# Picking the first expert's rows with matrix products instead of a gather, and loading the sink values without their zeros

## The chip, the cores and the metric

The kernel runs on one core of one Trainium2 chip. The metric is the device time of one execution in microseconds, from the first to the last instruction of the program with what the device adds around them. Each engine works through its own list of instructions in order: TensorE (PE), VectorE (DVE), ScalarE (ACT), GpSimd (POOL), and SyncE (SP), which only issues transfers.

## The reference

Three stages follow each other, and each one's output is the next one's input.

```python
# attention: B=2, H=8, S=768, D=64; 4 sink positions, window 128
scores = scale * np.matmul(q, k.transpose(0, 1, 3, 2))
keep = is_sink | in_window
scores = np.where(keep, scores, -1000000000.0)
a = softmax(scores);  attn_out = np.matmul(a, v)          # -> x, 1536 tokens x 512
# mixture of experts with a capacity: E=8, cap = 1536 // 8 = 192
logits = x @ w_gate
order = np.argsort(-logits.flatten())
for idx in order:
    tok, e = (int(idx) // E, int(idx) % E)
    if assigned[tok] >= 0 or counts[e] >= cap:
        continue
    assigned[tok] = e
    counts[e] += 1
for e in range(E):
    mask = assigned == e
    out[mask] = np.maximum(x[mask] @ w1[e], 0.0) @ w2[e]  # 512 -> 1024 -> 512
# dense layer over all tokens: 512 -> 2048 -> 512, w_in and w_out given in float64
h = x @ w_in
g = np.maximum(h, 0.0) + alpha * np.minimum(h, 0.0)
return (g @ w_out).astype(np.float32)
```

## The kernel before

**Who sets the order.** Every piece of work is a `task` of a planner (`Plan`) with a cost for each engine that may do it, what it reads and writes, and extra urgency (`urge`, `boost`). The planner simulates the engines, starts the most pressing ready task, and so writes out each engine's fixed order before the kernel is built. `lag` and `tail` are delays it assumes. Buffers come from rings (`Ring`); a task that wants a buffer waits until the last user of one is done.

**Attention.** 1536 tokens are 12 blocks of 128 (6 per batch element). The values lie in `vraw` (12 blocks of 128x512 float32, from `v` in four loads). Before a batch element's values can be used, the largest absolute value of its six blocks is taken, one block at a time (`vmax`): by ACT at L407 for the blocks in `BY_ACT`, else by DVE at L409. From it comes a power-of-two scale `svf` (and its inverse `isv`), and the values are split into a float16 high part and a float16 rest. The values of the four sinks arrive as `vsr`, laid out with one 65-wide column group per head on a block diagonal that is mostly zeros, and are split at L454 (ACT) and L458 (DVE). Each finished block of attention output `x` goes to DRAM (`xd`) and, scaled and split into `x16` (float16 high and rest, a ring of two buffers), to a transposed copy for the gate; the last two blocks (`TURNED`) are turned by TensorE instead, and split at L619 (ACT) and L621 (DVE).

**Routing.** It goes one expert after the other, `s` = 0 to 7. A phase (`closing`, then `phase`) finds each token's best expert left (row maximum `m`, L1067; one-hot `oh`, L1071), spreads the row maxima over all partitions (12 TensorE transposes of a broadcast column, L1096, copied by ACT at L1100), compares all tokens with all (`cm`, L1116 to L1131, in phase 1 for three blocks in a lent buffer that the trace calls `gt`; some of the comparisons start on ACT or POOL at L1121 and are finished by DVE at L1127 and L1131), and counts with TensorE (L1163, 144 products of 8 columns for 12 blocks). The threshold follows (`both`, `red`, transposes `total` at L1182), then the ranks `rk` and the tokens that are gone. Phase 0 runs inside attention, in two groups of blocks. The phases are chained: each takes the tokens that the one before left.

**Fetching an expert's rows** (`hot`, `gather`). DVE writes a one-hot table `ohs` of the expert's 192 places over the 12 blocks of tokens (L1266, 12 instructions of 128x192, float16). For experts 0 and 1, TensorE multiplies it with the token numbers (`tok`, one column each, L1425), DVE turns the sums into integers `sidx` (L1439, L1440), and POOL issues two indirect transfers that fetch the 192 rows from `xd` into `xg` (L1446). TensorE turns them (8 transposes, L1459) and ACT copies them to `xT` (L1463). `busy` (L1356) and `keep_busy` put products of 512 columns without use into the time in which TensorE waits for expert 0's rows: three of them and six.

**The rest.** An expert's first layer is 8 products of 4 matmuls (L1574, float32, which the trace lists as two rows each; `raw` are its weights), its second layer eight more of the same form; experts 4 to 7 use float16 parts (L1581). After every second expert comes a share of the dense layer (`chunk`, L1708 and L1751). Its weights w_in and w_out arrive as float64 bits in a ring of three (`r`), and are turned into float32 `w` in 34 buffers by ACT, DVE and POOL, a conveyor that runs from the routing on.

## Time and profile before

| | |
|---|---|
| runs | 609.23, 609.66, 613.13 us; median 609.66 us |
| profiled execution | 608.75 us; its span 607.0 us |
| mean granted clock of TensorE | 0.955 of full speed |
| PE busy | 559.9 us (92%), 4532 matmuls; weight loads beside them 410.0 us (68%) |
| DVE busy | 461.2 us (76%), 1299 instructions |
| ACT busy | 357.7 us (59%), 742 instructions |
| POOL busy | 161.0 us (27%), 247 instructions |

The shares are means over stages that differ: attention until about 97 us, the routing of the first two experts with the first expert's products until about 176 us, and from then on experts and dense layer. So the tables by stage and the chains of waits say more than the shares.

### The profile page before, as it was taken

The page shows a single profiled execution, that of the slowest core. Times are in us where ns is not written, and L with a number is a line of the kernel's source. Part 1 is how long each engine was busy: PE and PEld are TensorE (multiplying, and loading weights), DVE is VectorE, ACT ScalarE, POOL GpSimd, SP SyncE. Part 2 cuts the span into 40 slices and gives each one's busy share as a digit, 9 for nine tenths or more (in the row PEclk, how much of TensorE's full clock was granted, in tenths as well). Part 3 has the DMA queues.
Part 4 walks back from the last instruction along what each step waited for, and adds up shares of the span by engine and source line. Part 5 has one row for each costly group of instructions (what it writes and reads, how often), then busy time and mean ns, then how long its engine had stood idle before and what let it go on. Part 6 is the DMA issues. An engine that isn't in the chain of part 4 may idle for free.

```text
span 607.0 us, 12432 instructions
## 1 busy us (share of the span) xinstructions
PE 559.9 (92%) x4532; PEld 410.0 (68%) x4532; DVE 461.2 (76%) x1299; ACT 357.7 (59%) x742; POOL 161.0 (27%) x247
## 2 busy tenths in 40 slices
PE   5899997659789999999899999999999999899995
PEld 3567675449688668888898555598755559855552
DVE  6989987858647898998699998989987657743231
ACT  6778888357457967866665553566344446542222
POOL 4867835230643321436301201000220000020002
PEclk9789998569889999999999999999999999999998
DMA  8845354264868536343554448464697155210001
GB/s 282 295 104 134 100 87 140 50 219 116 305 183 280 205 105 209 97 138 107 153 164 157 131 144 309 164 195 153 196 321 256 39 169 166 80 43 10 1 0 53
DMA packets 40555, 91.99 MB, mean 152 GB/s; under 512 B 16703, under 2 KB 17230, under 8 KB 40398
## 3 DMA queue, kind: packets, MB, share of 16 engines
q1 hardware_dynamic: 37710, 84.27, 44.3%
q0 software_dynamic: 2784, 6.93, 3.3%
q8 instruction: 36, 0.59, 0.4%
q14 instruction: 25, 0.20, 0.1%
HBM read 82.15 MB, written 6.41 MB: 146 GB/s over the span
## 4 chain that ended last, share of the span: by engine, by line
PE 47%; issue 12%; DVE 11%; ACT 8%; DMA 4%; POOL 1%; another core or an unknown queue 0%; POOLq 0%; SPq 0%; ACTq 0%
PE o L1751 14%; PE h L1708 13%; PE h L1574 8%; PE h L1581 8%; DMA xg<-xd,sidx 3%; DVE spl L1559 1%; DVE cm L1116 1%; PE r L1163 1%; DVE cm L1131 1%; ACT w L860 1%; PE r L1459 1%; ACT spl L1557 1%; ACT cm L1121 1%; DVE w L900 1%; DMA L<-cd 1%
## 5 line engine op out<-in xcount | busy, mean ns | idle before, releaser
L1751 PE MATMUL o<-w,gt 128*128 128x512 f16 x432 | 101.9, 379 | 0.0
L1708 PE MATMUL h<-x,w 128*128 128x384 f16 x576 | 100.7, 326 | 0.0
L1708 PEld LDWEIGHTS <-w 128*128 128x128 f16 x576 | 55.8, 98 | 40.6 <-issue 0.5
L1721 ACT ACTIVATE t<-h,slope 128x384 f32<-128x384 f32 x64 | 37.0, 578 | 72.3 <-PE h L1708 72.2
L1751 PEld LDWEIGHTS <-gt 128*128 128x128 f16 x432 | 41.3, 98 | 43.3 <-issue 0.5
L1581 PEld LDWEIGHTS <-spl 128*128 128x128 f16 x768 | 63.4, 98 | 3.2 <-issue 2.6
L1724 DVE SCALAR_TENSOR_TENSOR v<-h,way,t 128x384 f32<-128x384 f32 x61 | 37.3, 612 | 35.3 <-ACT t L1721 35.3
L907 POOL TENSOR_TENSOR w<-w,sg 128x512 f32<-128x512 f32 x22 | 28.8, 1310 | 88.8 <-DVE w L900 29.0
L1574 PE MATMUL h<-xT,raw 128*128 128x192 f32 x256 | 48.1, 338 | 2.3 <-DVE x L1625 1.8
L1446 POOL DMA_INDIRECT xg<-xd,sidx x16 | 20.6, 1286 | 100.5 <-DVE sidx L1440 62.4
L1574 PE MATMUL h<-h,raw 128*128 128x192 f32 x256 | 46.4, 339 | 0.4 <-DVE x L1625 0.4
L506 ACT ACTIVATE P<-sm,mn 128x260 f32<-128x260 f32 (+1 forms) x96 | 42.7, 491 | 4.7 <-DVE mn L495 4.6
L1797 POOL DMA_INDIRECT out<-ot,sidx x9 | 8.9, 990 | 136.2 <-ACT ot L1788 97.4
L1574 PEld LDWEIGHTS h<-xT,raw 128*128 128x128 f32 x256 | 42.5, 194 | 3.4 <-DVE x L1625 2.1
L1574 PEld LDWEIGHTS h<-h,raw 128*128 128x128 f32 x256 | 43.5, 198 | 1.1 <-DVE x L1625 0.6
L1559 DVE SCALAR_TENSOR_TENSOR spl<-raw,es,spl 128x1024 f16<-128x1024 f32 x32 | 40.7, 1280 | 4.5 <-ACT spl L1557 4.4
L1728 ACT CAST gt<-v 128x384 f16<-128x384 f32 x48 | 24.5, 510 | 28.9 <-DVE v L1724 27.5
L485 PE MATMUL s<-k,q 64*128 64x260 f32 (+1 forms) x192 | 36.8, 457 | 4.4 <-DMA q<-qT 4.1
L495 DVE CUSTOM_DVE_ANT_0 sm<-s,mask 128x260 f32<-128x260 f32 (+1 forms) x96 | 35.7, 397 | 4.1 <-PE s L485 3.8
L1729 DVE TENSOR_TENSOR gt<-v,gt 128x384 f16<-128x384 f32 x48 | 26.5, 553 | 13.7 <-ACT gt L1728 13.6
L1557 ACT ACTIVATE spl<-raw,es 128x1024 f16<-128x1024 f32 x32 | 36.4, 1143 | 0.0
L1581 PE MATMUL h<-xT,spl 128*128 128x192 f16 x384 | 33.5, 246 | 1.5 <-DVE h L1604 1.2
(291 smaller groups left out, 1241.5 us busy)
## 6 DMA issues: line engine op xcount, KB each, us to landing
raw<-w SPq DMA_DIRECT2D x96, 512.0 KB, 4.6
r<-w_in SPq DMA_DIRECT2D x16, 512.0 KB, 8.1
r<-w_out SPq DMA_DIRECT2D x16, 512.0 KB, 4.4
vraw<-v SPq DMA_DIRECT2D x4, 768.0 KB, 8.5
xd<-x SPq DMA_DIRECT2D x12, 256.0 KB
k<-kT SPq DMA_DIRECT2D x11, 260.0 KB
q<-qT SPq DMA_DIRECT2D x11, 256.0 KB, 2.8
vsr<-vs SPq DMA_DIRECT2D x1, 780.0 KB
```

What stands on the lines that cost most here:

```text
L485: nc.tensor.matmul(s.tile[:, :n].rearrange("p (j k) -> p j k", k=KW), lhsT=qs[t].tile[half, p], rhs=kk, start=True, stop=True)
L495: task({"DVE": dve(n)}, lambda: nc.vector.tensor_tensor_reduce(out=sm.tile[:, :n], in0=s.tile[:, :n], in1=mask[:, :n], scale=-0.125, scala ...
L506: task({"ACT": act(n) + 0.137}, lambda h=h, sm=sm, mn=mn: nc.scalar.activation(P[t].tile[:, h, :n], sm.tile[:, :n], AF.Exp, bias=mn.tile, ...
L907: (nc.gpsimd if e == "POOL" else nc.vector).tensor_tensor(x.tile, x.tile, sg.tile, OP.mult)
L1557: task({"ACT": act_sb(1024) + 0.09}, lambda: nc.scalar.activation(v(0), src(), AF.Copy, scale=scale()), r=[raw, ws], w=[b.part(0)], lag=se ...
L1559: task({"DVE": dve(1024) + 0.2}, lambda: nc.vector.scalar_tensor_tensor(v(1), src(), scale(), v(0), OP.mult, OP.subtract), r=[raw, ws, b.p ...
L1574: nc.tensor.matmul(ps.tile[:, 0:CAP], lhsT=w[:, k], rhs=x, start=first and k == 0, stop=last and k == 3, skip_group_check=True)
L1581: nc.tensor.matmul(ps.tile[:, 0:CAP], lhsT=w[:, i, k], rhs=xs()[k][:, j], start=first and n == 0, stop=last and n == len(ways) - 1, skip_g ...
L1708: nc.tensor.matmul(ps.tile[:, 0:CH], lhsT=w[:, i, k], rhs=y[j][:, k], start=(n == 0), stop=(n == len(ways) - 1))
L1721: task({"ACT": act(CH)}, lambda: nc.scalar.activation(t.tile, ps.tile[:, 0:CH], AF.Copy, scale=slope), r=[ps, wres], w=[t])
L1724: task({"DVE": dve(CH) + 0.065}, lambda: nc.vector.scalar_tensor_tensor(to(), ps.tile[:, 0:CH], way, t.tile, OP.mult, OP.max), r=[ps, t, w ...
L1751: nc.tensor.matmul(ops[t].tile, lhsT=gv[:, i, sl], rhs=wv[:, j], start=(f == n == 0), stop=(f == FB - 1 and n == 2))
```

## The change

1. The value tile `vraw` outlives attention. Once a block's values are used up, its slot takes the float16 parts of that block's attention output, in place of the ring `x16`. The last two blocks, whose split went to the transposed copy alone, are split into their slots too (`lower`: L669 on ACT, L672 on DVE; the latter not before the comparisons of phase 0 are done).
2. Expert 0's rows are not gathered (`BY_PE`). 96 matmuls (L1444: weights 128x128 from `vraw`, the one-hot table of 192 columns as the moving side; 12 blocks x 2 parts x 4 column groups) add up in four banks of PSUM, two for each batch element, and L1454 (ACT, times `isv[0]`, then DVE, times `isv[1]` and added) writes `xT`. The index products of expert 0 stay, for the later scatter, with a delay of 20 us in the plan. The products without use go.
3. The sink values come without the zeros (`vs` 1/8 of the size) after the gate weights in SP's order (`ORDER`: k, q, two loads of values, w, s), and are spread on the chip with a mask `own` (a tensor product on DVE or POOL) after the split.
4. All twelve maxima of the values prefer ACT (`BY_ACT`).
5. Phase 1's row maxima and their broadcast get the urgency that phase 0's had (`soon`), expert 1's gather is planned with 4.0 us instead of 2.2 (`tail`).
6. The `w` ring takes 22 buffers of its own and the 12 slots of `vraw` once they are free (`lend`).

```diff
+class Kept(Buf):
...
+        self.tile = tile
...
+    def lend(self, kept):
+        self.pools += [k.tile for k in kept]
+        self.past += kept
...
-ORDER = "k q a b s w"
+ORDER = "k q a b w s"
...
-BY_ACT = (0, 1, 3)
+BY_ACT = tuple(range(12))
...
+def halves(tile):
+
+    return tile.bitcast(F16).rearrange("p (a d) -> p a d", a=2)
...
-    vraw = cst.tile([128, NBLK, DM], F32, name="vraw")
...
-    vsr = cst.tile([96, B, 2, H, D + 1], F32, name="vsr")
+    vsr = cst.tile([96, B, 2, D + 1], F32, name="vsr")
+    vsd = cst.tile([96, B, 2, D + 1], F16, name="vsd")
+    own = cst.tile([96, H], F16, name="own")
...
-    k_res, v_res = [Res() for _ in range(NBLK)], [Res() for _ in range(NBLK)]
+    k_res, v_res = [Res() for _ in range(NBLK)], [Kept(vraw[:, t]) for t in range(NBLK)]
...
-        load(lambda: nc.sync.dma_start(out=vsr, in_=vs), [vs_res], 1 << 19)
+        load(lambda: nc.sync.dma_start(out=vsr, in_=vs), [vs_res], 1 << 17)
...
+    own_res = Res()
+    task({"DVE": 0.2}, lambda: nc.vector.tensor_reduce(
+        own, ident[0:96, 0:96].rearrange("p (r h x) -> p h r x", r=3, h=H), AX.XY, OP.max), w=[own_res])
...
-            nc.scalar.activation(vsh[:, b, :, :, 0:D], vsr[:, b, :, :, 0:D], AF.Copy, scale=svf[b][0:96])
-            nc.scalar.copy(vsh[:, b, :, :, D:D + 1], vsr[:, b, :, :, D:D + 1])
-
-        task({"ACT": 1.1}, first, r=[vs_res, sv_res[b]], w=[vsh_res[b]])
-        task({"DVE": 1.15}, lambda: nc.vector.scalar_tensor_tensor(
-            vsh[64:96, b, :, :, 0:D], vsr[64:96, b, :, :, 0:D], svf[b][64:96], vsh[64:96, b, :, :, 0:D],
-            OP.mult, OP.subtract), r=[vs_res, sv_res[b]], w=[vsh_res[b]])
+            nc.scalar.activation(vsd[:, b, :, 0:D], vsr[:, b, :, 0:D], AF.Copy, scale=svf[b][0:96])
+            nc.scalar.copy(vsd[:, b, :, D:D + 1], vsr[:, b, :, D:D + 1])
+
+        def rest():
+            nc.vector.scalar_tensor_tensor(vsd[64:96, b, :, 0:D], vsr[64:96, b, :, 0:D], svf[b][64:96], vsd[64:96, b, :, 0:D],
+                                           OP.mult, OP.subtract)
+
+        def spread(e):
+            (nc.vector if e == "DVE" else nc.gpsimd).tensor_tensor(
+                vsh[:, b], vsd[:, b].unsqueeze(2).to_broadcast([96, 2, H, D + 1]),
+                own.unsqueeze(1).unsqueeze(3).to_broadcast([96, 2, H, D + 1]), OP.mult)
+
+        dense = Res()
+        task({"ACT": 0.4}, first, r=[vs_res, sv_res[b]], w=[dense])
+        task({"DVE": 0.25}, rest, r=[vs_res, sv_res[b]], w=[dense])
+        task({"POOL": 2.3, "DVE": 1.2}, spread, r=[dense, own_res], w=[vsh_res[b]])
...
-        task({"SP": 0.06}, lambda: nc.sync.dma_start(out=xd[block(t) * 128:(block(t) + 1) * 128, :], in_=x.tile), r=parts,
+        task({"SP": 0.06}, lambda: nc.sync.dma_start(out=xd[n * 128:(n + 1) * 128, :], in_=x.tile), r=parts,
...
+            late.append(lambda after: lower(t, after))
             return
-        x16, xs, xT = r_x16.new(), r_xs.new(), r_xT.new()
-        task({"ACT": 0.613}, lambda: nc.scalar.activation(x16.tile[:, 0], x.tile, AF.Copy, scale=svf[b]),
-             r=[*parts, sv_res[b]], w=[x16.part(0)])
+        x16 = lower(t)
+        task({"SP": 0.06}, lambda: nc.sync.dma_start_transpose(
+            out=xT.tile.rearrange("p a c k -> p (a c) k"), in_=x16.rearrange("p a d -> p (a d)")),
+            r=[v_res[n]], w=[xT.part(0), xT.part(1)], tail=2.8)
+
...
+        task({"ACT": 0.613}, lambda: nc.scalar.activation(x16[:, 0], x.tile, AF.Copy, scale=svf[b]),
+             r=[*parts, sv_res[b]], w=[own])
+        if t >= NBLK - TURNED:
+            task({"DVE": 0.67}, lambda: nc.vector.scalar_tensor_tensor(x16[:, 1], x.tile, svf[b], x16[:, 0], OP.mult, OP.subtract),
+                 r=parts, w=[own], after=after)
+            return
...
+        task({"POOL": 1.12}, lambda: nc.gpsimd.tensor_tensor(x16[:, 1], xs.tile, x16[:, 0], OP.subtract),
+             r=[xs], w=[own])
+        return x16
...
-                        vs[r, h, g, s, :, par, h, :D] = v[:, h, n, :]
+                        vs[r, h, g, s, :, par, :D] = v[:, h, n, :]
...
-        self.ring = Ring(ctx.enter_context(self.tc.tile_pool(name="w_cst", bufs=1)), "w", [128, DM], F32, 2 * FB + self.MORE)
+    def room(self, ctx, kept):
+        self.ring = Ring(ctx.enter_context(self.tc.tile_pool(name="w_cst", bufs=1)), "w", [128, DM], F32, 2 * FB + self.MORE - C)
+        self.ring.lend(kept)
...
-    FILL = 6
...
+    BY_PE = (0,)
+    PICK, SET = 300.0, 2000.0
...
-            soon = 2000.0 if s == 0 else 0.0
+            soon = 2000.0 if s == 0 else 2000.0 if s == 1 else 0.0
...
+        self.compared = task({"DVE": 0.35 * nb / C + 0.25}, thresholds, r=[*counted, far, *mm], w=[both, red])
+        seq.append(self.compared)
...
-        def keep_busy(after):
-
-            ps, last = r_h.new(), None
-            for _ in range(self.FILL):
-                last = task({"PE": 0.35}, lambda: nc.tensor.matmul(
-                    ps.tile, lhsT=self.ones, rhs=self.ones[:, 0:1].to_broadcast([128, 512]), start=True, stop=True,
-                    skip_group_check=True), w=[ps] if last is None else (), after=[last] if last else [after], boost=-1000.0)
...
+        def chosen(s, o, parts):
+            a = s % 2
+            xT = xTs[s] = r_xT.new()
+            banks = [[r.new() for h in range(2)] for r in (r_h, r_o)]
+            got = {(b, h): [] for b in range(2) for h in range(2)}
+            begun = set()
...
+                            b, rows = c // NB, halves(x16[c].tile)
+                            for k in range(2):
+                                for i in range(2):
+                                    at = (2 * h + k) * 128
+                                    nc.tensor.matmul(banks[b][h].tile[:, k * CAP:(k + 1) * CAP], lhsT=rows[:, i, at:at + 128],
+                                                     rhs=o.tile[:, c, a], start=(b, h) not in begun,
+                                                     stop=(c % NB == NB - 1 and k == i == 1), skip_group_check=True)
+                                    begun.add((b, h))
+
+                    task({"PE": 0.083 * 4 * len(cs)}, pick, r=[ro, *[x16[c] for c in cs]], w=[got[b, h][-1] for b in to], urge=self.PICK)
+            for h in range(2):
+                view = lambda b, h=h: banks[b][h].tile[:, 0:CH].rearrange("p (k t) -> p k t", k=2)
+                task({"ACT": act(CH)}, lambda h=h, v=view: nc.scalar.activation(
+                    xT.tile[:, 2 * h:2 * h + 2], v(0), AF.Copy, scale=isv[0]), r=[*got[0, h], sv_res[0]], w=[xT.part(h)], urge=self.SET)
+                task({"DVE": dve(CH) + 0.065}, lambda h=h, v=view: nc.vector.scalar_tensor_tensor(
+                    xT.tile[:, 2 * h:2 * h + 2], v(1), isv[1], xT.tile[:, 2 * h:2 * h + 2], OP.mult, OP.add),
...
-                             w=got[-1:], pre=busy(ips) if x == 0 else None)
-            if s == 0:
-                keep_busy(named)
...
+            if s in self.BY_PE:
+                chosen(s, o, parts)
...
+                    w=[to], tail=4.0 if s < 2 else 6.0)
             xT = xTs[s] = r_xT.new()
             src, pss = [], []
...
         L = logits[:, :, 0:E]
+        vraw = g.tile([128, C, DM], F32, name="vraw")
...
-            r_s, last = attention(tc, nc, plan, part, a["qT"], a["kT"], a["v"], a["vs"], a["wg"], xd, x_blocks, L, l_blocks,
-                                  n_sink, window, ident, identh)
-            routed.begin(part, r_s, GROUPS, [last])
+            r_s, last, late, x16, *back = attention(tc, nc, plan, part, a["qT"], a["kT"], a["v"], a["vs"], a["wg"], xd, x_blocks, L,
+                                              l_blocks, n_sink, window, ident, identh, g, vraw)
...
         weights.ways()
-        routed.build(ctx, a["w1"], a["w2"], weights, out)
```

On DVE, between the threshold of phase 0 and the one-hot table of expert 0, there stood before (`tot`, `mx`, `sm`, `ei`: the expert's total and name; `rf`, `rk`: ranks):

```order
L1203 TENSOR_TENSOR rf_2662<-qm_2648,sm_2654 128x96
L1204 TENSOR_REDUCE rk_2663<-rf_2662 128x12
L1210 SCALAR_TENSOR_TENSOR L<-sm_2654,L 128x12x8
L1208 SCALAR_TENSOR_TENSOR dead<-rk_2663,dead 128x12
L1266 TENSOR_SCALAR ohs_2726<-slots,rk_2663 128x192 x12
L1067 TENSOR_REDUCE m_2761<-L 128x12
L784 TENSOR_SCALAR way<-al 128x16
L785 TENSOR_SCALAR way<-way 128x16
L786 TENSOR_TENSOR slope<-way,al 128x16
L1070 SCALAR_TENSOR_TENSOR m_2776<-dead,m_2761 128x12
L1071 TENSOR_TENSOR oh_2777<-L,m_2776 128x96
```

and now, first where the threshold is formed, then at the table:

```order
L1239 SCALAR_TENSOR_TENSOR qm_2645<-oh_2257,s_2404 128x96
L672 SCALAR_TENSOR_TENSOR vraw<-x_2233,scv_167,vraw 128x512
L1231 TENSOR_REDUCE tot_2649<-s_2404 8x1
L672 SCALAR_TENSOR_TENSOR vraw<-x_2347,scv_167,vraw 128x512
L1083 TENSOR_REDUCE mx_2654<-s_2404 128x1
```

```order
L1258 SCALAR_TENSOR_TENSOR L<-sm_2653,L 128x12x8
L1256 SCALAR_TENSOR_TENSOR dead<-rk_2662,dead 128x12
L1114 TENSOR_REDUCE m_2725<-L 128x12
L1314 TENSOR_SCALAR ohs_2729<-slots,rk_2662 128x192 x4
L1117 SCALAR_TENSOR_TENSOR m_2739<-dead,m_2725 128x12
L1118 TENSOR_TENSOR oh_2740<-L,m_2739 128x96
L1314 TENSOR_SCALAR ohs_2729<-slots,rk_2662 128x192 x8
```

Two 128x512 operations have come in between the steps of the threshold, and phase 1's `m` and `oh` have moved ahead of the table's last eight blocks.

On PE, at the start of expert 0's rows, there stood the last index products, phase 1's broadcasts, six products without use (the last of the three before the index products stand further up), and then the turning of the gathered rows:

```order
L1425 MATMUL r_2737<-tok,ohs_2726 64x1
L1096 MATMUL r_2782<-ident,m_2761 128x128 x4
L1096 MATMUL r_2796<-ident,m_2761 128x128 x4
L1096 MATMUL r_2804<-ident,m_2761 128x128 x4
L1356 LDWEIGHTS ones
L1356 MATMUL h_2815<-ones 128x512
```

and now the broadcasts come right behind the threshold's last transpose, and the picks behind them:

```order
L1229 MATMUL s_2404<-ident,red_2641 8x128
L1233 MATMUL s_2404<-ident,tot_2649 128x8
L1143 MATMUL r_2734<-ident,m_2725 128x128 x4
L1143 MATMUL r_2743<-ident,m_2725 128x128 x4
L1143 MATMUL r_2757<-ident,m_2725 128x128 x4
L1444 LDWEIGHTS vraw
L1444 MATMUL h_2766<-ohs_2729,vraw 128x192
```

The 96 picks follow each other without anything between them, then 72 counts of phase 1 (L1210) ahead of expert 0's first product, where 36 stood before; L1454's two operations on DVE stand behind some twenty comparisons of phase 1 and conversions of `w`. The gathered rows of expert 1 are turned behind the first five products of expert 0's second layer, as before.

On ACT, early in attention, there stood before (`P`: the exponentials, `pth`: a copy of their transposes):

```order
L506 ACTIVATE P_340<-sm_325,mn_326 128x260
L407 ACTIVATE junk,mx<-vraw 128x512 x2
L506 ACTIVATE P_340<-sm_334,mn_335 128x260
L506 ACTIVATE P_340<-sm_342,mn_343 128x260
L506 ACTIVATE P_340<-sm_352,mn_353 128x260
L407 ACTIVATE junk,mx<-vraw 128x512
```

and now:

```order
L537 ACTIVATE P_343<-sm_328,mn_329 128x260
L429 ACTIVATE junk,mx<-vraw 128x512 x3
L537 ACTIVATE P_343<-sm_337,mn_338 128x260
L429 ACTIVATE junk,mx<-vraw 128x512 x3
L537 ACTIVATE P_343<-sm_345,mn_346 128x260
```

The eight maxima that DVE did have come to stand on ACT between the exponentials.

## Rows read from the trace of the kernel before

**Rows 1.** Table by stretch; columns: stretch, length, PE, PEld, DVE, ACT, POOL, PEclk, DMA, GB/s

```profile
10.00:30.00 20.00, 15.80 (x116) 10.07 (x114) 19.55 (x73) 15.93 (x37) 11.99 (x14) 0.84 0.90 302
119.00:137.00 18.00, 11.33 (x89) 8.92 (x89) 11.44 (x41) 8.69 (x15) 6.01 (x3) 0.59 0.58 197
161.00:176.00 15.00, 10.36 (x48) 9.97 (x47) 2.87 (x6) 4.32 (x11) 11.23 (x21) 0.77 0.57 190
205.00:290.00 85.00, 83.20 (x566) 68.14 (x565) 77.42 (x186) 60.64 (x128) 31.54 (x31) 1.00 0.41 128
```

**Rows 2.** The chain that ended last, 119 to 176 us; start, length, what

```profile
119.18 2.24 DVE ohs L1266 x12
...
123.19 10.41 DMA xg<-xd,sidx
133.64 2.09 PE h L1459 x8
...
136.68 2.77 PE h L1574 x8
...
146.54 1.41 PE h L1574 x8
...
156.75 7.78 DMA xg<-xd,sidx
164.57 1.76 PE r L1459 x7
166.32 9.34 PE h L1574 x40
```

**Rows 3.** Waits of PE, 100 to 200 us, and of DVE, from 119 us: us, times, longest

```profile
PE h L1459 <- DMA xg<-xd,sidx: 6.5, 1, 6.5
PE r L1459 <- DMA xg<-xd,sidx: 3.5, 1, 3.5
...
DVE gt L1127 <- ACT gt L1121: 5.3, 1, 5.3
```

**Rows 4.** Timeline of PE: start, length, instruction

```profile
122.62 2.96 PE L1096 MATMUL r<-ident,m 128*128 128x128 f32 x12
145.50 1.04 PE L1163 MATMUL r<-oh,cm 128*128 128x8 bf16 x36
153.44 0.54 PE L1425 MATMUL r<-tok,ohs 128*128 128x1 f16 x16
```

**Rows 5.** The chain that ended last, one stretch of float16 products near 419 us

```profile
419.22 12.04 PE h L1581 x144
```

**Rows 6.** Table of single microseconds, columns as in rows 1

```profile
122.00:123.00 1.00, 1.00 (x8) 0.93 (x8) 0.97 (x8) 0.66 (x1) 0.00 (x0) 0.50 0.99 401
126.00:127.00 1.00, 1.00 (x6) 0.29 (x3) 0.35 (x2) 1.00 (x3) 0.70 (x2) 1.00 0.93 340
138.00:139.00 1.00, 1.00 (x5) 1.00 (x4) 0.86 (x2) 1.00 (x1) 0.00 (x0) 0.50 0.00 0
140.00:141.00 1.00, 1.00 (x9) 0.94 (x8) 1.00 (x3) 1.00 (x1) 0.00 (x0) 1.00 0.00 0
```

**Rows 7.** Timeline of DVE, and one row of ACT's, 99 to 140 us

```profile
99.07 0.75 DVE L621 SCALAR_TENSOR_TENSOR xT<-pt,scv,xT 128x512 f16<-128x512 f32 x1 [0.17 <-ACT xT L619]
105.49 0.48 ACT L1100 COPY mrow<-s 128x384 f32<-128x384 f32 x1 [1.42 <-PE s L1096]
116.79 0.28 DVE L1184 TENSOR_REDUCE tot<-s 8x1 f32<-8x128 f32 x1 [0.47 <-PE s L1182]
139.78 0.35 DVE L1112 SCALAR_TENSOR_TENSOR gt<-mrow,m,tri 128x128 bf16<-128x128 f32 x1 [0.91 <-PE r L1163]
```

**Rows 8.** The maxima by their lines: ns of one (least, median, most), first and last start

```profile
L407 ACT ACTIVATE junk<-vraw x4: 615/619/631, 9.7 to 22.6; 128x512 f32<-128x512 f32 x4
L407 ACT ACTIVATION_READ_ACCUMULATOR junk<-vraw x4: 186/188/190, 10.2 to 23.1; 128x1 f32 x4
L409 DVE TENSOR_REDUCE mx<-vraw x8: 670/676/682, 10.4 to 23.0; 128x1 f32<-128x512 f32 x8
```

More of the change, by code (lines that the diff above doesn't have):

```diff
@@ L383, in pow2_scale @@
         m2 = cst.tile([128, 2], F32, name="m2" + name)
-        o = cst.tile([128, 4], I32, name="sc" + name)
+        o = keep.tile([128, 4], I32, name="sc" + name)
         a, b, c, ps = Res(), Res(), Res(), r_s.new()
@@ L711, in attention @@
     plan.chain(main)
-    return r_s, qks[-1]
+    return r_s, qks[-1], late, [v_res[block(t)] for t in range(NBLK)], isv, sv_res
 def lay_out_attention(inputs):
@@ L1879, in whole @@
         with ExitStack() as part:
-            r_s, last = attention(tc, nc, plan, part, a["qT"], a["kT"], a["v"], a["vs"], a["wg"], xd, x_blocks, L, l_blocks,
-                                  n_sink, window, ident, identh)
-            routed.begin(part, r_s, GROUPS, [last])
+            r_s, last, late, x16, *back = attention(tc, nc, plan, part, a["qT"], a["kT"], a["v"], a["vs"], a["wg"], xd, x_blocks, L,
+                                              l_blocks, n_sink, window, ident, identh, g, vraw)
+            compared = routed.begin(part, r_s, GROUPS, [last])
+            for f in late:
+                f([compared])
             plan.run()
-        weights.room(ctx)
+        weights.room(ctx, x16)
         weights.load_alpha()
         weights.ways()
-        routed.build(ctx, a["w1"], a["w2"], weights, out)
+        routed.build(ctx, a["w1"], a["w2"], weights, out, x16, *back)
         plan.run()
```

57 lines of the change are left out of this document (33 added, 24 removed).

## The prediction, made before the result was known

> **What bounds the kernel now.** I read the table by stretch first [rows 1]. From 205 us on PE is busy 83.2 of 85 us at full clock: there the kernel is as long as PE's work, and the change takes none of that away. From 10 to 30 us DVE is busy 19.55 of 20, PE 15.8. Between 119 and 137 PE has work for 11.33 of 18 us at a mean clock of 0.59, between 161 and 176 for 10.36 of 15 at 0.77. So the change can win in two places: the start of attention, and the routing of the first two experts.
>
> For the second place I followed the chain of waits [rows 2]. Expert 0's one-hot table starts at 119.18, its rows travel until 133.6, their turning takes 2.09 and its first product starts at 136.68. The routing of expert 1 ends in a second gather that lands at 164.53; 1.76 of turning and five products of expert 1 (9.34 us, until 175.66) follow. The waits [rows 3] say who stood still: PE 6.5 us for the first gather and 3.5 for the second (so it was done with expert 0's work before that at about 161.0), and DVE once 5.3 us for ACT, whose comparison for a lent buffer stands in ACT's order behind the copies of the first gather's rows. **The first gather thus holds up expert 1's routing as well, and that is the longer of two paths:** products reach 161.0, routing 164.5. A saving on the first alone is worth nothing.
>
> **Part 1: picks instead of the gather.** The gather and its eight transposes go; twelve broadcasts, which PE did at 122.62, come first, then 96 picks.
> - Start. DVE has the threshold done at 119.1 [rows 2], plus 0.6 for the new operations there (part 2) and 0.3 for phase 1's maxima: broadcasts from 120.05, 2.96 us at half clock [rows 4], until 123.0. The table, interrupted for phase 1's one-hot, is complete at about 122.6, in time.
> - Length of the picks. The trace has products of this form, 128x192 in float16 with new weights for each: 144 in 12.04 us, 83.6 ns each at full clock [rows 5]. So 96 take 8.0 us at full clock and 16.0 at half. The clock was 0.50 at 122 us and 1.00 at 126 [rows 6], after broadcasts and a few of the products without use. Picks begin where those began; I take a third of them at half clock (estimate): 10.7 us, until 133.7.
> - What follows. 72 counts of phase 1 at 29 ns (36 in 1.04 [rows 4]) keep PE until 135.8. `xT` needs two copies by DVE, with a conversion of `w` between; each is no wider than the 512 columns that took 0.75 [rows 7], so at most 2.25 us: 136.0. They stand behind some twenty comparisons, but those have from 123 on, and no longer wait for ACT behind a gather.
> - First product. At half clock it took 2.77 [rows 2] (the clock at 138 us was 0.50 [rows 6]), at full clock 1.41. It now ends at 136.0 + 1.41 = 137.4 instead of 139.45: -2.05. Behind it 36 counts less are due (-1.0), and 24 index products more (34 ns each [rows 4], +0.8). PE reaches the second gather at 161.0 - 2.25 = 158.8.
> - Expert 1's routing. The 5.3 us of DVE's wait go. Against them stand the copies and the conversion. At 136.0 DVE has done what it had done at 139.78 before [rows 7], where it starts the next comparison: 3.8 earlier. Ends: 1.0, if ACT's later comparisons or conversions take over the wait, and 5.3, if nothing does. Taken 3.8: the second gather lands at 160.7.
> - Afterwards PE waits 1.9 us instead of 3.5. Before, that wait was followed by work at half clock (mean 0.77 in [rows 1]); I take it that 1.9 us do not bring the clock down. Turning 0.9 instead of 1.76, five products 5 x 1.41 = 7.05 instead of 9.34: end at 160.75 + 0.9 + 7.05 = 168.7 instead of 175.66, **-7.0**. If the clock falls all the same, 3.8 is what remains. From there PE is the bound, so the gain stays.
>
> The Trainium skill, page "TensorE: Matmul & The Clock Gate", Part 4 (PE-mode transpose), says that transposes do not count as work for the clock in the way that matmuls do. The broadcasts are transposes, and no stretch of this trace has them alone ahead of a rise, so it leaves that open. By this rule the picks start cold; it is rival 3.
>
> **Part 2: the rest of the blocks' parts.** Ten blocks had their float16 parts made before; only the place changes. The last two cost two more ACT and two more DVE operations. ACT waits 1.42 us just there for the second group's broadcast [rows 7], which covers two such splits (0.62 each, as the maxima of the same 512 columns [rows 8]); without that cover they would cost 1.2 in phase 0. DVE's two take 0.75 each as L621's did, beside waits like the 0.47 before `tot` [rows 7], of which there are two: 1.5 - 0.94, +0.6 (ends 0 and 1.5), counted above.
>
> **Part 3: attention's start.** Eight maxima go from DVE (0.676 each, 5.4 us) to ACT (0.62 + 0.19 each, 6.5 us) [rows 8], all in the 10 to 23 us where DVE is full and ACT has 4.07 of 20 us free [rows 1]. The sink values' dense split spares ACT at least 2 x 0.6; DVE gets a mask and two small splits more (0.25 each, 0.8 in sum, bounded by the 0.28 of 128 columns in [rows 7]), and the spread replaces a split of about the same width. So DVE is relieved of 4.6, and ACT would need 15.93 + 6.5 - 1.2 = 21.2 of 20 us. One engine at its limit replaces the other. Ends: -4.6 (DVE alone set the pace) and +2.4 (ACT's excess without the sparing); taken 0. The smaller transfer of sink values (699 KB less, 2.3 us at the 302 GB/s of [rows 1]) frees the queue; I count it at nothing, because loads of values and keys stand ahead of it in either order. If it had held up the first products, up to 2.3 would come on top.
>
> By the rows, a maximum costs 0.13 us more on ACT than on DVE. The Trainium skill, page "ScalarE: Activation LUTs", Rules for kernel authors, wants max on VectorE, not ScalarE. The trace agrees on the price; by the rule alone the move costs 8 x 0.13 = 1.0 us.
>
> **Part 4: edits at nothing.** The lent buffers of `w` are free once the picks are done (133.7), and 22 others serve until then. The useless products filled waits. `tail` only moves expert 1's turning in the plan, and it stands behind five products in both orders.
>
> **The sum.** 608.75 - 7.0 = 601.75 for the profiled execution. The median of the runs is 0.91 above it: **602.7 us**.
>
> **Rivals.**
> 1. *The second gather lands no earlier.* DVE's wait moves to another place of the chain (ACT's comparisons, or `w` conversions waiting for a load), or the transfer, 7.78 us [rows 2], takes longer beside the weights. Then PE waits 5.7 us there instead of 3.5, at half clock afterwards as before: no gain, 609.7. For it: routing was the longer path all along. Against: the named wait of 5.3 us has its cause in the gather that goes.
> 2. *Attention's start gains too:* between half of DVE's 4.6 us and all of it, 598.1 to 600.4. For it: DVE's 19.55 of 20. Against: ACT's 21.2.
> 3. *The picks start cold.* Two thirds of them at half clock: 13.4 us, 2.7 later, and DVE's copies and the comparisons behind them as much. The second gather lands at 163.4, the five products end at 171.3 instead of 175.66: 605.3.
> 4. *Slower: the picks' weight loads do not hide.* All that follows waits for their end, the copies and, by the counts that free comparison buffers, the routing. My path ends at 168.7, 7.0 before the old one, so the change loses from picks of 10.7 + 7.0 = 17.7 us, 184 ns each. Weight loads take 0.12 us each in [rows 1] (68.14 us for 565); unhidden, a pick would take 205 ns, 19.6 us in all, and the time would be 611.6, at half clock more. Against it: the 144 products of [rows 5] also have a load each and hide it.
> 5. *It doesn't do what it says:* the picks run, but the plan's new order costs as much elsewhere: within 1%.
>
> **How the numbers follow.** Chances: forecast 0.48 (600 to 606, down to where the clock falls again), rival 1 0.15, rival 2 0.15, rival 3 0.12, rival 4 0.06, rival 5 0.04. About 1%, 6.1 us, is what a measurement of this kernel can tell from no change, so faster by that means under 603.6: some six tenths of the forecast, rival 2 whole, a quarter of rival 3 and a little of the upper gain: 0.52. Slower, over 615.8: part of rival 4 and of attention's +2.4 with no gain behind it, 0.06. The rest, 0.42, within 1%. The range from 597.5 to 610.0 takes in the forecast, rival 1 to 3 and the ends of part 3, and leaves out rival 4 and the tails.
>
> **What the profile after would show.** The table by stretch from 119 to 137: PE nearly full, and the clock at 1.00 from about 128. The picks' row: some 111 ns each in the mean, 10.7 us in all. First product of expert 0 before 136.5, 1.41 us. No wait of DVE for ACT of over 2 us between 125 and 140. Second gather landing by 161, PE's wait for it under 2.5 us, clock 1.00 from 161 to 170. From 10 to 30 us: DVE under 16, ACT 19 or more. The prediction is wrong if the second gather still lands at 164, if the picks take over 13 us, or if the start of attention moves by over 2 us either way.

## The result, and the profile after

The changed kernel took 602.5 us in the median of six runs, the kernel before 609.44 us in six on the same chip. The ratio, from paired rounds, is 0.9863 with a 95% interval of 0.9825 to 0.9902: 8.3 us less, 6.0 to 10.7 (the two medians by themselves differ by 6.9). The execution profiled with this result was a disturbed, slow one (609.81 us), so the rows below are from a second profile of the same kernel (`e0_changed_again`, 607.13 us, span 605.4). That is the longest of its six runs (598.53 to 607.13), so the rows show where steps moved and not the whole gain.

The table by stretch of the changed kernel (columns as in [rows 1]):

```profile
10.00:30.00 20.00, 17.62 (x106) 10.95 (x105) 13.89 (x67) 16.80 (x45) 8.74 (x11) 1.00 0.70 257
119.00:137.00 18.00, 16.93 (x205) 16.15 (x204) 16.49 (x51) 13.45 (x20) 1.16 (x1) 0.78 0.57 193
161.00:176.00 15.00, 9.49 (x45) 9.04 (x46) 5.59 (x11) 6.28 (x15) 10.16 (x17) 0.85 0.65 210
205.00:290.00 85.00, 84.92 (x580) 70.96 (x579) 78.13 (x202) 58.30 (x123) 30.00 (x32) 1.00 0.42 125
```

From 119 to 137 us PE is busy 16.93 of 18, where it was 11.33 [rows 1]. From 161 to 176 it is busy for less time than before, 9.49 against 10.36. The start is relieved: DVE 13.89 of 20 us instead of 19.55.

The chain that ended last of the changed kernel, 122 to 153 us (start, length, what):

```profile
122.78 5.44 PE h L1444 x40
128.23 0.66 PE o L1444 x8
128.89 0.66 PE h L1444 x8
129.55 3.30 PE o L1444 x40
132.85 1.78 PE r L1210 x72
134.63 1.41 PE h L1645 x8
...
140.59 1.41 PE h L1645 x8
...
142.11 0.81 PE r L1495 x8
142.92 1.50 PE h L1645 x8
...
144.57 1.84 PE r L1495 x16
146.41 4.27 PE h L1645 x16
150.68 0.19 PE r L1495 x8
150.87 1.52 PE h L1645 x8
152.39 0.39 PE r L1495 x16
...
152.80 0.04 DVE sidx L1504
```

The picks (L1444, 96) run back to back for 10.06 us of the chain (10.26 from the first start to the last end), then the counts and the first product of expert 0 at full speed. From 140 us on, look at what stands between the index products (L1495, 24 of expert 0 until 146.41, then 24 of expert 1): expert 0's products (L1645). The 48 take 3.2 us in sum, and the last of them ends at 152.78; most of that stretch is not theirs.

Single microseconds of the changed kernel (columns as in [rows 1]):

```profile
126.00:127.00 1.00, 1.00 (x8) 0.95 (x7) 1.00 (x3) 1.00 (x2) 0.00 (x0) 0.50 0.13 53
127.00:128.00 1.00, 1.00 (x14) 0.99 (x13) 1.00 (x5) 1.00 (x2) 0.00 (x0) 0.96 0.01 4
...
147.00:148.00 1.00, 1.00 (x7) 1.00 (x6) 1.00 (x8) 0.00 (x0) 0.00 (x0) 0.78 0.07 29
148.00:149.00 1.00, 1.00 (x5) 1.00 (x4) 1.00 (x7) 0.33 (x1) 0.00 (x0) 0.50 0.00 0
...
165.00:166.00 1.00, 1.00 (x4) 1.00 (x4) 0.00 (x0) 0.96 (x3) 0.81 (x2) 0.50 0.87 339
```

Between 147 and 151 us the granted clock falls to half, right behind the narrow index products; the 16 rows of expert 0's products that stand there (two products) take 4.27 us in the chain above.

The timeline of the changed kernel, DVE, POOL and PE (start, length, instruction, wait before it). `both` is the first step after a phase's counts, so the first row stands for the threshold of phase 0 and the second for that of phase 1:

```profile
114.04 0.26 DVE L1222 SCALAR_TENSOR_TENSOR both<-s,far 128x96 f32<-128x96 f32 x1 [0.55 <-PE s L1210]
140.65 0.25 DVE L1222 SCALAR_TENSOR_TENSOR both<-r,far 128x96 f32<-128x96 f32 x1
...
153.85 1.39 POOL L1517 DMA_INDIRECT xg<-xd,sidx  x1 [10.01 <-DVE w L947]
...
161.58 0.30 PE L1530 MATMUL r<-ident,xg 128*128 128x128 f32 x1 [1.82 <-DVE w L952]
163.90 1.10 PE L1530 MATMUL r<-ident,xg 128*128 128x128 f32 x7 [2.01 <-DMA xg<-xd,sidx]
...
174.68 7.64 PE L1645 MATMUL h<-xT,raw 128*128 128x192 f32 x35 [2.92 <-DVE x L1696]
```

And three rows of the kernel before that answer to the first three (the first transfer of the second gather is the third):

```profile
115.25 0.26 DVE L1175 SCALAR_TENSOR_TENSOR both<-s,far 128x96 f32<-128x96 f32 x1 [0.65 <-PE s L1163]
146.66 0.25 DVE L1175 SCALAR_TENSOR_TENSOR both<-r,far 128x96 f32<-128x96 f32 x1
...
154.96 1.48 POOL L1446 DMA_INDIRECT xg<-xd,sidx  x1 [4.49 <-DVE ids L1298]
```

From threshold to threshold it is 26.6 us instead of 31.4: the picks brought phase 1 forward by 4.8. From the second threshold to the turning of the gathered rows it is 23.25 us instead of 17.9 [rows 2]: 5.3 lost. The gain of this stretch is made and given back inside it. The DVE and POOL timelines of the two kernels, and of a third profile of the changed one (`e4_changed_third_look`, below), divide the way from phase 1's threshold to the turning like this (us):

| from, to | before | changed, second profile | changed, third profile |
|---|---|---|---|
| threshold `both` to expert 1's total `mx` | 2.89 | 3.95 | 3.88 |
| `mx` to the ranks `rf` | 0.98 | 1.92 | 1.92 |
| `rf` to the integers `sidx` of expert 1 | 4.00 | 6.28 | 4.68 |
| `sidx` to the issue of the gather | 0.43 | 1.05 | 1.05 |
| issue to the turning of its last rows | 9.61 | 10.05 | 8.70 |
| sum | 17.91 | 23.25 | 20.23 |

### The profile page after: what moved, and what is told of

The parts are those of the page before. It is cut to its first block, busy times and chain, and to the rows that moved or that the text cites. A ratio compares the mean times of both kernels' runs of the same rounds, so it can differ in the third digit from the quotient of the medians.

```text
span 608.1 us, 12597 instructions
## 1 busy us (share of the span) xinstructions
PE 563.9 (93%) x4611; PEld 420.3 (69%) x4611; DVE 456.6 (75%) x1301; ACT 365.3 (60%) x762; POOL 152.0 (25%) x243
## 4 chain that ended last, share of the span: by engine, by line
PE 67%; issue 12%; DVE 10%; ACT 5%; DMA 3%; another core or an unknown queue 1%; POOL 1%; SPq 0%; POOLq 0%; ACTq 0%; DVEq 0%
PE o L1822 15%; PE h L1779 15%; PE h L1645 11%; PE h L1652 8%; PE s L516 4%; PE pt L551 3%; PE r L1210 2%; DVE spl L1630 1%; DVE cm L1178 1%; DMA L<-cd 1%; DVE ptl L561 1%; PE h L1444 1%; PE pv L602 1%; DMA q<-qT 1%
## 5 line engine op out<-in xcount | busy, mean ns | idle before, releaser
L1822 PE MATMUL o<-w,gt 128*128 128x512 f16 x324 | 76.5, 379 | 0.0
L1779 PE MATMUL h<-x,w 128*128 128x384 f16 x360 | 63.2, 326 | 0.0
L1645 PE MATMUL h<-xT,raw 128*128 128x192 f32 x256 | 51.0, 354 | 3.9 <-DVE x L1696 3.9
L1779 PEld LDWEIGHTS <-w 128*128 128x128 f16 x360 | 35.1, 98 | 25.7
L1645 PEld LDWEIGHTS h<-xT,raw 128*128 128x128 f32 x256 | 45.7, 206 | 4.7 <-DVE x L1696 4.2
L1645 PE MATMUL h<-h,raw 128*128 128x192 f32 x256 | 45.7, 336 | 0.0
L1645 PEld LDWEIGHTS h<-h,raw 128*128 128x128 f32 x256 | 43.1, 196 | 0.1
L1517 POOL DMA_INDIRECT xg<-xd,sidx x14 | 15.6, 1117 | 99.7 <-DVE sidx L1508 59.3
L516 PE MATMUL s<-k,q 64*128 64x260 f32 (+1 forms) x192 | 35.4, 464 | 5.3 <-DMA q<-qT 5.3
L1779 PE MATMUL h<-x,vraw 128*128 128x384 f16 x216 | 37.7, 326 | 0.0
L1800 DVE TENSOR_TENSOR gt<-v,gt 128x384 f16<-128x384 f32 x48 | 26.4, 553 | 13.9 <-ACT gt L1799 13.8
```

Source lines behind the costliest of these rows:

```text
L516: nc.tensor.matmul(s.tile[:, :n].rearrange("p (j k) -> p j k", k=KW), lhsT=qs[t].tile[half, p], rhs=kk, start=True, stop=True)
L1645: nc.tensor.matmul(ps.tile[:, 0:CAP], lhsT=w[:, k], rhs=x, start=first and k == 0, stop=last and k == 3, skip_group_check=True)
L1779: nc.tensor.matmul(ps.tile[:, 0:CH], lhsT=w[:, i, k], rhs=y[j][:, k], start=(n == 0), stop=(n == len(ways) - 1))
L1800: task({"DVE": dve(CH) + 0.1}, lambda: nc.vector.tensor_tensor(gview(gt)[:, 1], v.tile, gview(gt)[:, 0], OP.subtract), r=[v, gt.part(0)], ...
L1822: nc.tensor.matmul(ops[t].tile, lhsT=gv[:, i, sl], rhs=wv[:, j], start=(f == n == 0), stop=(f == FB - 1 and n == 2))
```

## The experiments

Each time is the ratio to the kernel before on the same chip with its 95% interval, and the same in microseconds of 609.4. All kernels compute the whole reference.

**The same kernel again** (no edit).

> The changed kernel once more, for a closer time and an undisturbed profile. By the forecast: 7.0 us below the kernel before, ratio 0.9885, all of it between 119 and 176 us of the span; picks 10.7 us, first product of expert 0 at the full clock's 1.41 us, expert 1's gather landed by 161. By rival 1 (the second gather lands no earlier) the time between 119 and 205 us is unchanged and any gain must stand elsewhere.

Measured: 0.988 [0.9835, 0.9925], -7.3 us. The rows above are its. In what follows, a distance to the changed kernel is one to this -7.3.

**The gather again for expert 0, all else as changed.**

```diff
-    BY_PE = (0,)
+    BY_PE = ()
```

> The changed kernel with expert 0's rows gathered by the transfers again (BY_PE empty), all else as changed. If the picks carry the gain (forecast), the time returns to 609 to 611, a ratio to the kernel before of 1.00 within 0.5%. If attention's start, the dense sink values or the earlier row maxima carry it (rival 2), it stays at 602 to 606.

Measured: 1.0117 [1.0056, 1.0177], +7.1 us. The timeline of POOL and PE:

```profile
126.97 3.20 POOL L1517 DMA_INDIRECT xg<-xd,sidx  x1 [3.95 <-DVE cm L1163]
130.48 9.40 POOL L1517 DMA_INDIRECT xg<-xd,sidx  x1 [0.30 <-DVE gt L1178]
...
144.44 1.76 PE L1530 MATMUL h<-ident,xg 128*128 128x128 f32 x7 [11.32 <-DMA xg<-xd,sidx]
```

PE waits 11.32 us for this gather, where the kernel before waited 6.5 [rows 3]: the second half was issued in 9.40 us, and the useless products that filled this wait are gone from the code. It came out above both forecasts. The changed plan needs the picks, then; but a gather in a plan made for picks is not the gather of before, so the 14 us to the changed kernel are not what the picks gain.

**The start as before: order of loads and maxima put back, dense sinks and picks kept.**

```diff
-ORDER = "k q a b w s"
+ORDER = "k q a b s w"
-BY_ACT = tuple(range(12))
+BY_ACT = (0, 1, 3)
```

> The changed kernel with the start of attention as before (maxima on DVE but for three blocks, sink values ahead of the gate weights; the sink values stay dense). Forecast: attention's start is worth nothing, 602.5 within 1.5 us. Rival 2: 2.3 to 4.6 us of the gain go, 605 to 607.

Measured: 0.9989 [0.996, 1.0019], -0.7 us (-2.4 to +1.2). Its timeline:

```profile
116.22 0.26 DVE L1222 SCALAR_TENSOR_TENSOR both<-s,far 128x96 f32<-128x96 f32 x1 [0.64 <-PE s L1210]
142.76 0.25 DVE L1222 SCALAR_TENSOR_TENSOR both<-r,far 128x96 f32<-128x96 f32 x1
...
165.53 0.98 PE L1530 MATMUL r<-ident,xg 128*128 128x128 f32 x7 [1.99 <-DMA xg<-xd,sidx]
```

26.5 us between the thresholds and 22.8 to the rows, as in the changed kernel. So the -7.0 of part 1 is refuted: with the old order and maxima, picks, urgency and dense sinks together bring 2.4 us at most.

**The start alone: dense sinks, order and maxima put into the kernel before.** The edit is the change's hunks for `vs`, `vsd`, `own`, the split and the spread, with the two lines above turned the other way round; the gather stays.

```diff
-    vsr = cst.tile([96, B, 2, H, D + 1], F32, name="vsr")
+    vsr = cst.tile([96, B, 2, D + 1], F32, name="vsr")
+    vsd = cst.tile([96, B, 2, D + 1], F16, name="vsd")
+    own = cst.tile([96, H], F16, name="own")
```

> The kernel before with all of the change to attention's start (dense sink values spread on the chip, order of loads, maxima on ScalarE), and the gather, the queue orders' costs and the buffers as before. If the start is worth some 5 us by itself: ratio to the kernel before 0.990 to 0.993. If it is worth something only together with the picks, or through the order that the plan makes of it: ratio 0.998 to 1.002.

Measured: 0.9915 [0.9884, 0.9947], -5.2 us (-7.1 to -3.2). The table by stretch of its first microseconds:

```profile
10.00:30.00 20.00, 17.31 (x141) 10.93 (x139) 16.86 (x80) 19.62 (x53) 10.52 (x13) 1.00 0.75 268
```

And its timeline of DVE and PE:

```profile
110.60 0.26 DVE L1189 SCALAR_TENSOR_TENSOR both<-s,far 128x96 f32<-128x96 f32 x1 [0.55 <-PE s L1177]
...
141.19 0.25 DVE L1189 SCALAR_TENSOR_TENSOR both<-r,far 128x96 f32<-128x96 f32 x1
...
158.35 1.75 PE L1473 MATMUL r<-ident,xg 128*128 128x128 f32 x7 [3.00 <-DMA xg<-xd,sidx]
```

The threshold of phase 0 comes at 110.60 instead of 115.25, 4.65 earlier, and what is behind keeps its old distance to within 0.8 us a step: 30.6 us to the next threshold (31.4 before), 17.2 to the rows (17.9 before). Nothing but the start was edited, so the whole gain of this kernel is the start's. One profile can't give its size, for the same kernel's first threshold moves by some 3 us between executions (last section); but over all profiles it came at 110.6 to 115.2 us in the eight kernels and executions with the whole new start, and at 115.3, 116.2 and 117.9 in the three with the old order and maxima. ACT is full here (19.62 of 20), as reckoned, and the change pays all the same.

**Which piece of the start.** Three kernels: the maxima alone in the kernel before; the changed kernel with only its maxima put back; the changed kernel with only its order of loads put back.

```diff
-BY_ACT = (0, 1, 3)
+BY_ACT = tuple(range(12))
```

> The kernel before with one edit, all twelve maxima prefer ScalarE. Forecast: no difference, ratio 1.00 within 0.3%. Rival 2: 2.3 to 4.6 us faster, ratio 0.9925 to 0.996. If ScalarE's excess of load decides instead, up to 2.4 us slower, ratio 1.004.

Measured: 1.002 [0.9989, 1.005], +1.2 us (-0.7 to +3.0). From 10 to 30 us DVE is relieved here as well (17.16 us busy instead of 19.55) and ACT is full (19.50); nothing comes of it.

```diff
-BY_ACT = tuple(range(12))
+BY_ACT = (0, 1, 3)
```

> The changed kernel with the maxima of values where they were (VectorE but for three blocks), the order of loads as changed. Undoing maxima and order together cost 5.6 us. If the maxima carry that: 605 to 608. If the order of loads does, or the two only together: 601 to 604.

Measured: 0.9922 [0.9891, 0.9954], -4.8 us.

```diff
-ORDER = "k q a b w s"
+ORDER = "k q a b s w"
```

> The changed kernel with the sink values ahead of the gate weights in SyncE's order as before, the maxima as changed. If the order of loads carries the 5.6 us: 605 to 608. If the maxima do: 601 to 604.

Measured: 0.9903 [0.9864, 0.9941], -5.9 us.

With dense sinks and picks in place, either of the two edits alone is enough for most of the gain (-4.8 with the order alone, -5.9 with the maxima alone, -0.7 with neither), and the second adds 1.4 to 2.5 us, within the intervals. The maxima without the dense sinks bring nothing, and the dense sinks with neither edit (the kernel with the start as before) next to nothing: it takes the dense sinks and one of the two edits. What the dense sinks, or the order, bring by themselves in the kernel before wasn't run, so how the 5 us divide, and whether it is DVE's work or the 699 KB less to load, stays open.

**The picks alone, with the plan's urgency and delay of before.** The start as before, and

```diff
-            soon = 2000.0 if s == 0 else 2000.0 if s == 1 else 0.0
+            soon = 2000.0 if s == 0 else 0.0
-                    w=[to], tail=4.0 if s < 2 else 6.0)
+                    w=[to], tail=2.2 if s < 2 else 6.0)
```

> The changed kernel with the start of attention as before, and phase 1's row maxima without the added urgency and the gather's planned time of 2.2 us as before; what stays is the picks, the kept buffers and the dense sink values. If the picks alone carry the gain: 602 to 604. If the start of attention carries some 5 us of it, as its taking away did: 606 to 609. If the earlier row maxima count too: over 609.

Measured: 1.0189 [1.0139, 1.0239], +11.5 us. Its timeline:

```profile
117.85 0.26 DVE L1222 SCALAR_TENSOR_TENSOR both<-s,far 128x96 f32<-128x96 f32 x1 [0.65 <-PE s L1210]
155.81 0.26 DVE L1222 SCALAR_TENSOR_TENSOR both<-r,far 128x96 f32<-128x96 f32 x1 [1.93 <-PE r L1210]
```

38.0 us between the thresholds against 26.5 with the two numbers of the change. Picks without the two numbers that let phase 1 go first cost 12 us; which of the two it is wasn't tried. In this order the broadcasts stand behind the picks:

```profile
122.41 5.28 PE L1444 MATMUL h<-ohs,vraw 128*128 128x192 f16 x40 [2.31 <-DVE ohs L1314]
```

The granted clock was at half when these picks began too, and rose at about 126.2, 3.8 us into them.

**Longer picks.** One more product of 128 columns behind each pick, into columns that nothing reads.

```diff
+                                    nc.tensor.matmul(banks[b][h].tile[:, 2 * CAP:512], lhsT=rows[:, i, at:at + 128],
+                                                     rhs=o.tile[:, c, a, 0:128], start=False,
...
```

> The changed kernel with one more product of 128 columns behind each pick, into a part of the banks that nobody reads: 96 more, 5.4 us by columns at the picks' rate of 84 ns for 192, more if weight loads do not hide. If the picks stand on the path that sets the end (forecast: what follows waits for their end): 5 us slower or more, 607 to 610. If the second gather's landing is set by something else (the transfers of weights, or index products behind expert 0's products on TensorE): under 2 us slower.

Measured: 0.9969 [0.9905, 1.0033], -1.9 us, that is 5.4 behind the changed kernel, with intervals that overlap. The ratio rests on the three shortest of its ten runs; the median of the ten is 613.3 us, 2.2 above that of the kernel before beside them. The timeline:

```profile
114.54 0.26 DVE L1222 SCALAR_TENSOR_TENSOR both<-s,far 128x96 f32<-128x96 f32 x1 [0.55 <-PE s L1210]
146.15 0.26 DVE L1222 SCALAR_TENSOR_TENSOR both<-r,far 128x96 f32<-128x96 f32 x1
```

The picks end at 138.32 instead of 132.84, 5.5 us later, and the threshold of phase 1 comes 5.5 later (0.5 of both is this execution's start). So the picks' length is on the path to expert 1's routing, and nothing hides it up to there.

**Expert 1's index products first.** The changed plan assumes a delay of 20 us for expert 0's index products, which keeps them out of the picks' way. Here 60, and urgency for expert 1's.

```diff
-                             w=got[-1:], lag=20.0 if s in self.BY_PE else 0.0)
+                             w=got[-1:], urge=400.0 if s == 1 else 0.0, lag=60.0 if s in self.BY_PE else 0.0)
```

> The changed kernel with expert 1's index products urgent and expert 0's planned 40 us later. In the profile expert 0's index products stand between the steps of phase 1 on TensorE and an integer copy of theirs on VectorE ahead of phase 1's ranks, and eat most of a lead of 6 us. If that holds the second gather: it is issued 2 to 3 us earlier and the time falls by 1 to 3 us, to 599 to 601. If the landing is set by the full transfer queues: no change.

Measured: 1.034 [1.0283, 1.0397], +20.7 us. The timeline of POOL:

```profile
188.81 1.02 POOL L1517 DMA_INDIRECT xg<-xd,sidx  x1
```

The gather was issued at 188.81: the planner had put POOL's transfers for the next phase and conversions of `w` ahead of it. So it says nothing of PE's order, which was its question.

**The same with a small step:** 25 instead of 20.

```diff
-                             w=got[-1:], lag=20.0 if s in self.BY_PE else 0.0)
+                             w=got[-1:], lag=25.0 if s in self.BY_PE else 0.0)
```

> The changed kernel with expert 0's index products planned 25 us later instead of 20. On TensorE they then stand behind the last step of phase 1's threshold and not between its steps, VectorE's copy of them behind phase 1's ranks, and GpSimd still issues the second gather ahead of the compaction's transfers. If these products hold back the second gather: issued 2 to 3 us earlier than at 153.9, and 1 to 3 us off the time. If the full transfer queues set its landing: no change.

Measured: 1.0014 [0.9979, 1.0049], +0.9 us, 8 behind the changed kernel. The timeline of PE and POOL:

```profile
143.48 4.17 PE L1645 MATMUL h<-xT,raw 128*128 128x192 f32 x24
147.48 2.58 PE L1495 MATMUL r<-tok,ohs 128*128 128x1 f16 x40
...
153.58 1.21 POOL L1517 DMA_INDIRECT xg<-xd,sidx  x1 [2.30 <-DVE w L945]
```

Index products still stand behind three of expert 0's products, and the gather is issued 0.27 earlier only. It does land earlier (rows turned from 160.51 instead of 163.90), and the kernel is slower nevertheless: from 280 to 295 us PE is busy 11.28 of 15, in the changed kernel all 15. A gather that lands 3.4 earlier did not carry through to the end. Of the first half of the expectation the DVE timeline shows what it says: with expert 0's index products out from between the steps of the threshold, these two steps take 2.94 and 1.19 us, close to the kernel before (2.89 and 0.98). But the third, from the ranks to the integers of expert 1, takes 7.73: the same products now stand there, among expert 1's.

**A third profile of the changed kernel.**

> The changed kernel a third time, for its profile alone. Theory one (the gain is time that TensorE no longer spends idle or at half clock between 119 and 176 us, and later): picks 10.0 us, first product of expert 0 near 134.5 at 1.41 us, phase 1's threshold near 141 instead of 146.7, the second gather landing at 163 to 164. Theory two (what differs between executions lies in the start of attention): the time from 0 to phase 0's threshold differs by 2 us or more from the 114.0 and 115.2 us of the two looks before.

Measured: 604.30 us; threshold 0 at 111.79, threshold 1 at 138.18 (26.4 between), the rows at 158.41 (20.2). Theory two's sign is there: the first threshold is over 2 us earlier than in the two profiles before. The lead between the thresholds is there in all three; how much of it is lost behind the second threshold differs, 2.3 us here against 5.3. PE's order is the same, and the chain shows one thing that differs (start, length, what):

```profile
142.02 1.84 PE r L1495 x16
143.86 2.80 PE h L1645 x16
```

Here the clock stays at 1.00 from 142 to 160 us, and the same 16 rows take 2.80 us instead of 4.27. Its 10 to 30 us differ as well:

```profile
10.00:30.00 20.00, 15.30 (x156) 10.47 (x155) 17.78 (x83) 19.75 (x53) 11.67 (x17) 1.00 0.79 273
```

## Why the prediction came out as it did

The number was right to 0.2 us by the medians and to 1.4 by the ratio, and for the wrong reason: two terms were mis-sized, and by luck their errors cancel.

**Part 1, picks: right.** 10.26 us were measured for 10.7 forecast, 107 ns each for 111. The clock rose at 127.1 us, 4.5 us into the picks, so a little less than the third at half clock that was taken; rival 3, with two thirds, did not come about. The first product took 1.41 and ended at 136.04; forecast 137.4, and 1.2 of the difference is the start of this execution. Rival 4 is refuted: at full clock the chain shows 40 picks in 3.30 us, 83 ns, weight loads hidden.

The Trainium skill, page "TensorE: Matmul & The Clock Gate", Part 4 (PE-mode transpose), would have transposes not count for the clock. The runs do not contradict it: in the nine profiles with the broadcasts right ahead of the picks, the clock was at half when the broadcasts ended and came up 2.2 to 5.1 us into the picks. But PE also stood idle around the broadcasts (2.37 and 1.07 us in the second profile), and in the profile without broadcasts ahead the clock came up 3.8 us into the picks, so it can't be told here whether it was the transposes or the idle time that left the picks cold.

**Part 1, phase 1's threshold: right.** The wait of 5.3 us [rows 3] is gone (the longest of DVE's waits from 125 to 140 us is 0.2), and, counted from the first threshold, the second came 4.8 earlier against the 3.8 taken.

**Part 1, the step that failed: "the second gather lands at 160.7".** It landed at 163.9 (by 164.5 before). The step carried DVE's lead through to the gather as if nothing but the 24 index products, 0.8 us, lay between. But PE works in order: the change put expert 0's index products, with their delay of 20 us, between the steps of phase 1's threshold, and the plan set expert 0's products, in whole groups of 1.4 us, between the routing's small products. DVE's own waits in the trace of the changed kernel show it:

```profile
DVE sidx L1504 <- PE r L1495: 2.3, 1, 2.3
DVE mx L1083 <- PE r L1233: 1.8, 1, 1.8
DVE sidx L1508 <- PE r L1495: 0.9, 1, 0.9
```

In order of time: `mx` waits for the total over the partitions, which stands behind 8 of expert 0's index products and a group of its products (1.8); the integers of expert 0, which stand ahead of expert 1's ranks on DVE, wait for the other 16 of its index products (0.9); the integers of expert 1 wait for its index products, which stand behind two groups and then one (2.3). That is 5.0 us of waiting, but not all of it is loss: in the kernel before, a group stood ahead of the total as well, and DVE converted `w` meanwhile. By the table above, the three steps cost 1.1, 0.9 and 2.3 us more than before, 4.3 of the 5.3; 0.6 more passes before the issue and 0.4 in the transfer.

The first two, 2.0, go with expert 0's index products: with the delay of 25 they are gone. The third is only in part PE's order: in the third profile, with the same order at full clock, DVE waits 0.75 us there and not 2.3, and the step costs 0.7 more than before. So of the 5.3 some 2.7 are the order on PE, 1.6 the clock that fell to half at 147.6 us, and the rest the issue and the transfer. The forecast had neither that order nor this fall of the clock in its sum.

The term of 0.8 us for 24 more index products was mis-read, too. It takes 34 ns each from expert 1's row in [rows 4]; the products that come in are expert 0's, and the 24 of these took 2.65 us (0.81 and 1.84 in the chain), 110 ns each. They had taken 3.19 us in the kernel before, at half clock:

```profile
119.51 3.19 PE L1425 MATMUL r<-tok,ohs 128*128 128x1 f16 x24
```

With them and the stretch at half clock, PE is done with expert 0's work ahead of the second gather at 159.77, no earlier than before (159.80, which the prediction read as 161.0 because it left out a first wait of 1.0 before the first turning), although its first product ended 3.4 earlier. PE then waits 1.82 us before the first turning and 2.01 before the others (1.00 and 3.47 before), and the clock is at half by 165, which the forecast took not to happen. After four products of expert 1 comes a wait of 2.92 us for DVE's `x` (1.85 before). The fifth product starts at 174.68 and so ends at about 176.1, where it ended at 175.66 [rows 2]. This is rival 1, and it won in its stage, by a way it did not name: not ACT, `w` or the transfer, but PE's own order and its clock.

So part 1, -7.0 in the sum, measured -0.7 (-2.4 to +1.2) without the new order and maxima, and by difference -2.1 beside the start (-7.3 less -5.2, or -3.1 with the first result's -8.3; the intervals overlap). Whether a part of the lead comes back later isn't shown: from 205 to 290 us PE is busy 84.92 against 83.20 [rows 1], but from 205 to 600 us the two are level, 388.19 against 388.30.

**Part 3, the other failing step: "taken 0".** It measured -5.2 (-7.1 to -3.2). The ends named, -4.6 and +2.4, were set by who is full; the lower one was met, so what rival 2 said of the start came true in whole (its time, 598.1 to 600.4, did not, because part 1 failed). ACT does become the full engine (19.62 of 20 in the kernel with the start alone), but the kernel does not pay for its excess. The reason that the prediction gave for its lower end, DVE alone setting the pace, isn't shown for all that: with the maxima alone DVE was relieved too, and nothing was gained. The signs named for 10 to 30 us hang on the execution: DVE 13.89 and ACT 16.80 in the second profile, 17.78 and 19.75 in the third, where "DVE under 16" and "ACT 19 or more" were expected.

The Trainium skill, page "ScalarE: Activation LUTs", Rules for kernel authors, would have max on VectorE. For the maxima alone the runs do not contradict it (+1.2, -0.7 to +3.0, beside the 1.0 worked out from the rows' prices), but with dense sinks, picks and the old order the same move is worth 5.2 us (-5.9 against -0.7). There the measurement decides: the engine that is slower by the instruction was the right one. Why isn't shown; from 10 to 30 us VectorE was busy 17.89 us with the maxima and 16.12 without, so not full in either.

**Part 2 and part 4.** No run tells part 2 from nothing; in the trace DVE needs 0.4 us more than before from the first threshold to the mark of the tokens that are gone (4.26 against 3.88), where +0.6 was taken. Part 4's nothing for `tail` isn't shown: put back together with the urgency, it is part of 12 us. Rival 5 ("costs as much elsewhere") describes the stretch from 140 to 165 well, but not the kernel.

## What to carry to other kernels

A lead that is won on one engine reaches the next stage only if no in-order engine on the way has been given more work by the same change; so follow each small instruction of the critical path through the order of its queue, not only through its duration, and take its price from a row of the same instruction at the same place: 34 ns and 110 ns were both in these traces. When work moves from a full engine to one that would then be full too, take the two ends as equally likely instead of zero, and measure that part alone in the kernel before: one such run here took the sum apart. And where a planner sets the order, an edit comes with the plan's numbers: 12 us hung on an urgency and a delay, 8 us on five microseconds of an assumed delay.

## What the runs showed of the hardware

The issue of one indirect transfer of the gather by POOL took 1.0 to 1.5 us in most places, 3.40 for the first transfer of the first gather of the kernel before, and 3.20 and 9.40 us in the kernel with the gather put back. In the latter both lie where DVE is working through 16-bit comparisons; that is a coincidence in time, and no run varied it alone.

The granted clock need not be the same in two executions of one program at the same place: behind expert 0's 24 index products of one column it fell from 1.00 to 0.50 at 147.6 us in the second profile and stayed at 1.00 in the third, which made 1.5 us of difference for two products.

The same program does not start the same way twice: the threshold of phase 0 came at 115.18, 114.04 and 111.79 us in three profiled executions. One profile therefore can't tell a start that is 2 us better.
